# Exponentials written over the scores in PSUM, longer rings for halves and turned halves, w_out converted amid layer 1: cluster attention with two feed-forward layers on one core

## The chip, the cores and the metric

The kernel runs on one core of a Trainium2 chip. The metric is the device time of one execution in microseconds; the median of three runs stands for the kernel. A profiled execution is one more run with the hardware profiler on.

## What is computed

Attention in which a query sees only the keys of its own cluster, then a feed-forward layer with SiLU, then a second one with PReLU. Sizes: 2 batches, 8 heads, 768 rows, 64 columns a head, 16 clusters; the 1536 rows of 512 then pass through 512 x 2048 and 2048 x 512 twice. The weights arrive as 8-byte floats.

```python
q_assign = np.argmax(np.einsum('bhsd,hcd->bhsc', q_n, c_n), axis=-1)   # q_n, c_n: rows of length one
k_assign = np.argmax(np.einsum('bhsd,hcd->bhsc', k_n, c_n), axis=-1)
scores = scale * np.matmul(q, k.transpose(0, 1, 3, 2))
scores = np.where(q_assign[:, :, :, None] == k_assign[:, :, None, :], scores, -1000000000.0)
attn = np.exp(scores - np.max(scores, axis=-1, keepdims=True))
x = np.matmul(attn / (np.sum(attn, axis=-1, keepdims=True) + 1e-09), v)  # then heads side by side
h = x @ w_in;   x = (h * (1.0 / (1.0 + np.exp(-h)))) @ w_out             # first layer
h = x @ w2_in;  out = (np.maximum(h, 0.0) + alpha * np.minimum(h, 0.0)) @ w2_out
```

## The kernel before

Every number that enters a matmul is kept as two halves of 16 bits, a high and a low one, and each product is made of three matmuls (high by high, high by low, low by high).

Attention runs in 96 units, one for each tile of 128 rows and head: twelve tiles, eight heads. `front(u)` makes one unit's scores with four matmuls into one of two score buffers in PSUM (`bank_s`, two banks each; L804, L808). VectorE scales them in place and finds the extreme value (L818), ScalarE takes the exponential into one of two SBUF buffers of `p_buf` (L823), copies it to a high half (L830), and VectorE subtracts for the low half (L832; the list `P_LO_DVE` names the units that VectorE serves, all 96). The halves lie in one of two buffers (`o_hl`). `front_t(u)` has the DMA queue on SyncE turn them (L838) into one of three buffers (`o_pt`, `NPT`). `back(u)` multiplies them with the values (L850, 18 matmuls a unit, into `bank_x`). It is traced `LAG` units behind `front`, 2 here. After a tile's eighth unit `x_done` divides, splits and turns the tile's result (L870 to L881).

The first layer runs in seven chunks of one or two tiles (`CHUNKS`). `layer1(c)` makes eight groups of 24 matmuls against w_in (L1202), each with a Tanh on ScalarE (L1209) and passes of both engines behind it (L1210 to L1214), and then four groups of 48 matmuls against w_out (L1233). These groups take the two `w` banks of PSUM in turn; a third bank, `m`, joins once `w2_start` has been traced. Each weight is loaded in eight pieces, converted from 8-byte floats (L915 to L929), squared and summed (for the first layer by TensorE into a `w` bank, L964, read at L966), scaled by a common power of two (sums at L507, then L1048) and split into halves (L941, L942).

Weight preparation stands in a queue of tasks (`bg`). For the first layer it holds twelve tasks for w_in, four loads and eight conversions for w_out; `W_TASKS[u]` of them are traced behind unit u. `w1_finish` traces the rest, with w_out's scale and splits; it is called at step `W1_OUT_AT` = 16 of the first chunk. `UNITS_FIRST` says how many units are traced before the first chunk of layer 1; `UNITS_BY_CHUNK` how far attention has been traced at the end of each chunk. When all `NU + LAG` units are traced, `w2_start` queues the preparation of the second layer's weights, one task a step; their raw buffers lie where the keys were.

The order in which this is traced is not the order in which it runs. `Plan` takes all instructions with a cost for each and the data dependences between them (a PSUM tile counts as one cell), tries 61 orders with a seeded noise, and the one with the earliest end by its own count becomes the fixed order on every engine. What the traced order fixes is which buffer each use takes, and so which use has to wait for which.

Of the kernel before, what the change touches and what calls it, by code (L numbers as in the profile page):

```python
# [11 lines left out]
F32 = mybir.dt.float32  # L12
F16 = mybir.dt.float16
# [3 lines left out]
ACTF = mybir.ActivationFunctionType  # L17
ALU = mybir.AluOpType
# [3 lines left out]
CHUNKS = ((0, 1), (1, 1), (2, 2), (4, 2), (6, 2), (8, 2), (10, 2))  # L22


UNITS_FIRST = 17
UNITS_BY_CHUNK = (32, 53, 64, 69, 98, 98, 98)
W_TASKS = (
    2, 2, 2, 2, 1, 1, 1, 1, 2, 2, 2, 2, 2, 2, 2, 2,
    1, 1, 1, 1, 2, 2, 3, 2, 1, 1, 1, 1, 1, 1, 1, 1, 1, 1, 1, 1, 2, 2, 2, 2,
)  # L30
W2_TASKS = 1
W1_OUT_AT = 16
W_LOAD_AT = (0, 1, 3, 5)
# [5 lines left out]
V_SCALE_ON = ("papa", "appp")  # L39
SPLIT = ("aaaaaaaa", "aaaaaaaa", "aaaaaaaa", "aaaaaaaa")  # L40
EXP_ON = ("aaaaaaaa", "aaaaaaaa", "aaaaaaaa", "aaaaaaaa")
P_LO_DVE = range(96)

OUT_LAG = 2
READERS = 6
# [5 lines left out]
class Plan:  # L51
# [144 lines left out]

    def improve(self, rounds):

        noise = Random(3)
        found = [self.run(list(range(len(self.ins))))]  # L200
        back = self.mirror()
        for _ in range(rounds):
            back.run([noise.gauss(0, 0.1) - t for t in self.ended])
            found.append(self.run([noise.gauss(0, 0.1) - t for t in back.ended]))
        return min(found, key=lambda x: x[0])
# [128 lines left out]
def cluster_attention_silu_prelu(  # L334
# [20 lines left out]
    nc = tc.nc  # L355
    B, H, S, D = q.shape
# [7 lines left out]
    NC2 = 3  # L364
    N2 = NTILE * 128 // NC2

    NPT = 3
    NSTAT = 400
    NSCR = 128

# [1 line left out]
    KB = 1024  # L372
# [7 lines left out]
    def view(off, dt, *dims):  # L380
        n = 1
        for d in dims:
            n *= d
        nb = n * (2 if dt in (F16, BF16) else 4)
        assert off % 4 == 0 and nb % 4 == 0 and off + nb <= total, (off, nb)
        a = arena[:, off // 4:(off + nb) // 4]
        if dt != F32:
            a = a.bitcast(dt)
        if len(dims) == 1:
            return a  # L390
        names = [f"a{i}" for i in range(len(dims))]
        pat = f"p ({' '.join(names)}) -> p {' '.join(names)}"
        return a.rearrange(pat, **{n: d for n, d in zip(names, dims)})
# [3 lines left out]
    def region(nbytes):  # L397
        o = pos[0]
        pos[0] += nbytes
        return o  # L400
# [11 lines left out]
    o_qraw = region(4 * KB)  # L412
    o_kvraw = region(8 * KB)
    o_preq = region(4 * KB)
    o_p = region(6 * KB)
    o_hl = region(6 * KB)
    o_pt = region(NPT * 3 * KB)
    o_xhl = region(KB)
    o_xf = region(2 * KB)
# [13 lines left out]
    def col(n):  # L433
        a = stat[:, nstat[0]:nstat[0] + n]
        nstat[0] += n
        assert nstat[0] <= NSTAT
        return a
# [91 lines left out]
    def ring(name, n):  # L529
        i = ring_pos.get(name, 0)  # L530
        ring_pos[name] = i + 1
        return i % n

    def p_buf():
        return o_p + 3 * KB * ring("p", 2)


    half = small_p.tile([128, 12], F32, name="half")
    has = small_p.tile([128, B, H], F16, name="has")
# [60 lines left out]
    def load_kv(b, pr, which):  # L600
        return nc.sync.dma_start(
            out=view(kv_raw(b, pr)[which], F32, 2, T * D),
            in_=(k, v)[which][b, 2 * pr:2 * pr + 2].rearrange("h (p t) d -> p h (t d)", t=T),
        )
# [57 lines left out]
    def prep_v(b, pr):  # L662
        vr = view(kv_raw(b, pr)[1], F32, G, D)
        vt = view(o_v + 3 * KB * pr, F16, G, 2, D)
        nc.scalar.activation(out=vt[:, :, 0, :], in_=vr, func=ACTF.Copy)
        nc.gpsimd.tensor_tensor(out=vt[:, :, 1, :], in0=vr, in1=vt[:, :, 0, :], op=ALU.subtract)
        did.add(("v", b, pr))
        if pr == NP - 1:
            v_scales(b)
# [92 lines left out]
    def head_scales(n, pairs):  # L762

        b = n // T
        qt2 = view(o_qt + 4 * KB * (n % 2) + 2 * KB, F16, H, 128)
        d = d_cols[:, NP * (n % 2):NP * (n % 2) + NP]
        if pairs[0] == 0:
            (nc.gpsimd if n else nc.vector).tensor_scalar(
                d, isk[b], q_inv[:, n % 2:n % 2 + 1], 1.0 / float(D) ** 0.5 / MASK,
                op0=ALU.mult, op1=ALU.mult,  # L770
            )
        h0, nh = 2 * pairs[0], 2 * len(pairs)
        own = psum("m", nh)
        for i in range(nh):
            nc.tensor.matmul(
                out=own[:, i:i + 1], lhsT=qt2[0:D + C, h0 + i], rhs=has[0:D + C, b, h0 + i:h0 + i + 1],
                start=True, stop=True,
            )
        o = H * (n % 2) + h0
        nc.vector.tensor_tensor(  # L780
            out=nd_cols[:, o:o + nh].rearrange("p (a b) -> p a b", b=2),
            in0=own.rearrange("p (a b) -> p a b", b=2),
            in1=bc(d[:, pairs[0]:pairs[0] + len(pairs)], 2), op=ALU.mult,
        )
# [3 lines left out]
    sums = [col(H) for _ in range(2)]  # L788
# [5 lines left out]
    def front(u):  # L794
        n, h = divmod(u, H)
        b, pr = n // T, h // 2
        sc = bank_s[ring("s", 2)]
        qt1 = view(o_qt + 4 * KB * (n % 2), F16, H, 128)
        qt2 = view(o_qt + 4 * KB * (n % 2) + 2 * KB, F16, H, 128)
        kt1 = view(o_kt1 + 3 * KB * pr, F16, 2, T * 128)  # L800
        kt2 = view(o_kt2 + 3 * KB * pr, F16, 2, T * 128)
        hs = S // 2
        for j in range(2):
            nc.tensor.matmul(  # L804
                out=sc[:, j, :hs], lhsT=qt2[0:D + C, h],
                rhs=kt2[0:D + C, h % 2, j * hs:(j + 1) * hs], start=True, stop=False,
            )
            nc.tensor.matmul(  # L808
                out=sc[:, j, :hs], lhsT=qt1[:, h],
                rhs=kt1[:, h % 2, j * hs:(j + 1) * hs], start=False, stop=True,  # L810
            )
        if n % T == 0:
            if h % 2 == 0:
                head_scales(n, [pr])
        elif h == 0:
            head_scales(n, list(range(NP)))
        bias = un_cols[:, u % 3:u % 3 + 1]
        nc.vector.tensor_scalar(  # L818
            sc[:, :, :hs], sc[:, :, :hs], nd_cols[:, H * (n % 2) + h:H * (n % 2) + h + 1], None,
            op0=ALU.mult, op1=ALU.min, accum_out=bias,  # L820
        )
        o = p_buf()
        nc.scalar.activation(  # L823
            out=view(o, F32, 2, hs), in_=sc[:, :, :hs], func=ACTF.Exp, scale=-1.0, bias=bias,
            accum_out=sums[n % 2][:, h:h + 1],
        )
        p = view(o, F32, S)
        i = u % 2
        hl = view(o_hl + 3 * KB * i, F16, 2, S)
        nc.scalar.activation(out=hl[:, 0], in_=p, func=ACTF.Copy)  # L830
        en = nc.vector if u in P_LO_DVE else nc.gpsimd
        en.tensor_tensor(out=hl[:, 1], in0=p, in1=hl[:, 0], op=ALU.subtract)  # L832
        pt = view(o_pt + 3 * KB * (u % NPT), F16, 2 * T, 128)
        pt_of[u] = pt

    def front_t(u):
        hl = view(o_hl + 3 * KB * (u % 2), F16, 2 * S)
        nc.sync.dma_start_transpose(out=pt_of[u], in_=hl)  # L838

    def back(u):  # L840
# [221 lines left out]
    def run_bg(n):  # L1062
        for _ in range(n):
            if bg:
                bg.popleft()()
# [11 lines left out]
                f()  # L1077


    LAG = 2  # L1080
    NU = NTILE * H
    ready = set()
    g1_done = set()
# [1 line left out]
    def attention():  # L1085
# [36 lines left out]
        prep_v(0, 0)  # L1122
        for u in range(NU + LAG):
            n, h = divmod(u, H)
            if u < NU:
                front(u)
            if u >= LAG:
                back(u - LAG)
                if (u - LAG) % H == H - 1:
                    c = x_done((u - LAG) // H)  # L1130
                    if c is not None:
                        ready.add(c)
            if u < NU:
                front_t(u)
# [5 lines left out]
            for b in range(1, B):  # L1140
# [3 lines left out]
                for pr in range(NP):  # L1144
                    if at == (2 * pr - 2 if pr >= 2 else pr - 4):
                        load_kv(b, pr, 0)
                    if at == (2 * pr - 1 + LAG if pr else -2):
                        load_kv(b, pr, 1)
# [10 lines left out]
            if n + 1 < NTILE and n < NTILE:  # L1159
# [4 lines left out]
                if h == Q_AT[1]:  # L1164
                    prep_q_b(n + 1)
            run_bg(W_TASKS[u] if u < len(W_TASKS) else 0)
            yield u
# [365 lines left out]

    attend(UNITS_FIRST)
    while 0 not in ready:
        attend(done[0] + 1)
    steps = KF + 4 * KD
    for c in range(len(chunks)):
        while c not in ready:
            attend(done[0] + 1)  # L1540
        first = done[0]
        target = min(NU + LAG, UNITS_BY_CHUNK[c])
        steps_of = layer1(c)
        for i in range(steps):
            if c == 0:
                while i < KF and w1["in"].scales[i // 4] in bg:
                    run_bg(1)
                if i == W1_OUT_AT:
                    w1_finish()
            next(steps_of)  # L1550
            attend(first + (target - first) * (i + 1) // steps)
            if done[0] >= NU + LAG and not w2:
                w2_start()
            if w2:
                run_bg(W2_TASKS)
            if c == len(chunks) - 1 and i == KF + 4:
                split_x2(0)
        next(steps_of, None)
# [52 lines left out]
```

## Time and profile before

| | |
|---|---|
| median of 3 runs | 763.19 us (760.87 to 764.05) |
| the profiled execution | 764.79 us |
| its span, first to last instruction | 762.7 us |
| TensorE busy | 668.0 us (88%), 7035 matmuls |
| VectorE busy | 600.8 us (79%) |
| ScalarE busy | 483.8 us (63%) |
| GpSimd busy | 137.8 us (18%) |
| transposing DMAs | 149, median 3.9 us from issue to landing |
| loads of 8-byte weights | 32 of 1 MB, median 6.0 and 5.8 us to landing |

Busy time is not peak: matmuls are pipelined and their ends are modelled. A wait is put down to the releaser that came last by the profile. Idle time of an engine counts only where it is the one that the end waits for.

### The profile page before, as it was taken

How to read it: one execution, taken by the hardware profiler on the slowest of the kernel's cores; microseconds unless marked ns; L12 is line 12 of the kernel's file. 1: busy time of each engine (PE TensorE's matmuls, PEld its weight loads, DVE VectorE, ACT ScalarE, POOL GpSimd, SP SyncE). 2: the span in 40 equal slices, each digit the busy share in tenths (PEclk: the TensorE clock that was granted, in tenths of full speed). 3: DMA queues.
4: the chain of work that ended last, by engine and by line, in shares of the span. 5: the costliest groups of instructions: out<-in, count | busy, mean ns of one | idle time of the engine just before them, and what ended most of it. 6: DMA issues, size and time to landing. Idle time of an engine off the chain costs nothing.

```text
span 762.7 us, 17062 instructions
## 1 busy us (share of the span) xinstructions
PE 668.0 (88%) x7035; PEld 502.7 (66%) x7035; DVE 600.8 (79%) x1084; ACT 483.8 (63%) x779; POOL 137.8 (18%) x231
## 2 busy tenths in 40 slices
PE   0355568779999899999899999999999999999997
PEld 0243347668888788888788898884444687666653
DVE  4789999897679469867867885778999999966640
ACT  7978677877778557756765897888754532313111
POOL 4633042312232550321220101000000000000000
PEclk9995568899999999999999999999999999999999
DMA  7979997999989979988869875353200000001001
GB/s 223 315 191 271 295 274 156 143 164 162 180 161 160 151 139 161 157 155 141 146 117 149 191 176 137 146 214 126 111 1 0 28 28 1 2 1 56 1 0 56
DMA packets 237357, 100.86 MB, mean 132 GB/s; under 512 B 217312, under 2 KB 227552, under 8 KB 237280
## 3 DMA queue, kind: packets, MB, share of 16 engines
q1 hardware_dynamic: 237280, 99.78, 60.2%
q8 instruction: 55, 0.90, 0.5%
q14 instruction: 22, 0.18, 0.1%
HBM read 43.03 MB, written 3.15 MB: 61 GB/s over the span
## 4 chain that ended last, share of the span: by engine, by line
PE 41%; DVE 13%; DMA 9%; ACT 6%; issue 4%; POOL 1%; ACTq 0%; SPq 0%; POOLq 0%; DVEq 0%
PE s L1489 11%; PE w L1233 8%; PE w L1202 6%; PE w L1446 5%; DMA arena<-arena 4%; PE x L850 3%; DVE arena L942 3%; DMA arena<-in_moe_w_in_dram 3%; PE x L1446 2%; DMA arena<-in_moe_w_out_dram 2%; PE m L1446 2%; PE s L804 2%; PE s L808 2%; ACT arena L956 1%; DVE arena L1312 1%
## 5 line engine op out<-in xcount | busy, mean ns | idle before, releaser
L1233 PE MATMUL w<-arena 128*128 128x256 f16 (+1 forms) x1248 | 152.5, 259 | 5.2 <-DVE arena L942 4.3
L1202 PE MATMUL w<-arena 128*128 128x256 f16 (+1 forms) x1200 | 139.7, 258 | 2.7 <-DVE arena L1210 2.3
L1489 PE MATMUL s<-arena 128*128 128x512 f16 x576 | 134.3, 379 | 0.0
L1233 PEld LDWEIGHTS <-arena 128*128 128x128 f16 x1344 | 113.0, 99 | 24.0 <-DVE arena L942 5.2
L1202 PEld LDWEIGHTS <-arena 128*128 128x128 f16 x1344 | 113.4, 99 | 18.2 <-issue 3.9
L818 DVE TENSOR_SCALAR_CACHE_REDUCE s<-s,stat 128x768 f32<-128x768 f32 x96 | 97.9, 1021 | 21.4 <-PE s L808 15.1
L850 PE MATMUL x<-arena 128*128 128x64 f16 x1728 | 105.2, 198 | 7.6 <-DMA arena<-arena 7.6
L823 ACT ACTIVATE arena<-s,stat 128x768 f32<-128x768 f32 x96 | 86.0, 896 | 39.0 <-DVE s L818 19.9
L832 DVE TENSOR_TENSOR arena<-arena 128x768 f16<-128x768 f32 x96 | 94.6, 986 | 19.6 <-ACT arena L830 19.0
L850 PEld LDWEIGHTS <-arena 128*128 128x128 f16 x1728 | 88.7, 101 | 19.0 <-DMA arena<-arena 10.7
L1489 PEld LDWEIGHTS <-arena 128*128 128x128 f16 x576 | 56.3, 98 | 60.5
L830 ACT ACTIVATE arena<-arena 128x768 f16<-128x768 f32 x96 | 80.3, 839 | 21.7 <-DMA arena<-arena 21.3
L1406 ACT ACTIVATE arena<-arena,stat 128x512 f16<-128x512 f32 x48 | 33.7, 717 | 75.2 <-DVE arena L1403 75.1
L1446 PEld LDWEIGHTS <-arena 128*128 128x128 f16 x672 | 65.6, 98 | 15.6 <-issue 0.8
L804 PE MATMUL s<-arena 80*128 80x384 f16 x192 | 67.9, 356 | 8.3 <-ACT arena L823 5.7
L454 POOL TENSOR_SCALAR stat<-stat 128x1 int32<-128x1 int32 (+1 forms) x41 | 14.4, 355 | 324.8 <-DVE stat L449 220.5
L808 PE MATMUL s<-arena 128*128 128x384 f16 x192 | 68.1, 355 | 0.0
L942 DVE SCALAR_TENSOR_TENSOR arena<-arena,stat 128x1024 f16<-128x1024 f32 x40 | 51.5, 1306 | 9.0 <-ACT arena L941 9.0
L926 DVE SCALAR_TENSOR_TENSOR arena<-arena 128x1024 int32<-128x1024 int32 x32 | 39.2, 1224 | 24.6 <-ACT arena L919 24.5
L1446 PE MATMUL w<-arena 128*128 128x256 f16 x336 | 53.6, 273 | 0.4 <-ACT arena L1465 0.4
L941 ACT ACTIVATE arena<-arena,stat 128x1024 f16<-128x1024 f32 x40 | 45.7, 1173 | 11.2 <-DVE arena L1319 3.8
L915 ACT ACTIVATE arena<-arena 128x1024 int32<-128x1024 uint32 x32 | 36.8, 1151 | 22.2 <-DMA arena<-in_moe_w_out_dram 11.2
(176 smaller groups left out, 1076.6 us busy)
## 6 DMA issues: line engine op xcount, KB each, us to landing
arena<-in_moe_w_in_dram SPq DMA_DIRECT2D x16, 1024.0 KB, 6.0
arena<-in_moe_w_out_dram SPq DMA_DIRECT2D x16, 1024.0 KB, 5.8
arena<-in_k_dram SPq DMA_DIRECT2D x8, 384.0 KB, 3.9
arena<-in_q_dram SPq DMA_DIRECT2D x6, 512.0 KB, 5.5
arena<-in_v_dram SPq DMA_DIRECT2D x8, 384.0 KB, 6.2
out_dram<-arena SPq DMA_DIRECT2D x12, 256.0 KB, 2.1
arena<-arena SPq DMA_TRANSPOSE x149, 3.9
arena<-in_centroids_dram SPq DMA_DIRECT2D x1, 32.0 KB, 3.2
```

The costliest lines, as they stand in the source:

```text
L804: nc.tensor.matmul(out=sc[:, j, :hs], lhsT=qt2[0:D + C, h], rhs=kt2[0:D + C, h % 2, j * hs:(j + 1) * hs], start=True, stop=False,)
L808: nc.tensor.matmul(out=sc[:, j, :hs], lhsT=qt1[:, h], rhs=kt1[:, h % 2, j * hs:(j + 1) * hs], start=False, stop=True,)
L818: nc.vector.tensor_scalar(sc[:, :, :hs], sc[:, :, :hs], nd_cols[:, H * (n % 2) + h:H * (n % 2) + h + 1], None, op0=ALU.mult, op1=ALU.min, ...
L823: nc.scalar.activation(out=view(o, F32, 2, hs), in_=sc[:, :, :hs], func=ACTF.Exp, scale=-1.0, bias=bias, accum_out=sums[n % 2][:, h:h + 1],)
L830: nc.scalar.activation(out=hl[:, 0], in_=p, func=ACTF.Copy)
L832: en.tensor_tensor(out=hl[:, 1], in0=p, in1=hl[:, 0], op=ALU.subtract)
L850: nc.tensor.matmul(out=x_ps[0][:, h], lhsT=pt[:, ph * T + t], rhs=vt[:, h % 2, t, vh], start=(i == 0), stop=(i == 3 * T - 1),)
L942: nc.vector.scalar_tensor_tensor(out=lo, in0=t, scalar=s, in1=hi, op0=ALU.mult, op1=ALU.subtract)
L1202: nc.tensor.matmul(out=hp[:, ff], lhsT=wi[ff][:, a, kd], rhs=mov(bb, kd), start=(i == 0), stop=(i == 3 * KD - 1),)
L1233: nc.tensor.matmul(out=acc, lhsT=wo[:, a, f % 2, dt * 128:(dt + 1) * 128], rhs=g[:, f, bb], start=(i == 0), stop=(i == 3 * KF - 1),)
L1446: nc.tensor.matmul(out=hp[:, ff], lhsT=a_[:, a, kd, at + 128 * ff:at + 128 * ff + 128], rhs=b_[:, bb, kd], start=(k == 0), stop=(k == 5),)
L1489: nc.tensor.matmul(out=acc[t], lhsT=g[:, q, a, t * 128:(t + 1) * 128], rhs=wo[:, bb, f % 2], start=(first and q == 0 and k == 0), stop=(la ...
```

## The change

The buffers for exponentials go: the exponential is written over the scores in PSUM, and the copy and the subtraction read it there. There are three buffers for halves instead of two and four for turned halves instead of three; the value product is traced three units behind. The conversion of w_out is no longer traced during the first units: `W_TASKS` ends after ten units, with all of w_in and w_out's four loads, and the eight conversions follow one by one behind every second step of the first chunk's first half. That chunk is traced from unit 12 on instead of 17. The seed of the plan's noise is another. `UNITS_BY_CHUNK` stays, so that the last targets are 98 where all units traced make 99.

```diff
-UNITS_FIRST = 17
+UNITS_FIRST = 12
 UNITS_BY_CHUNK = (32, 53, 64, 69, 98, 98, 98)
-W_TASKS = (
-    2, 2, 2, 2, 1, 1, 1, 1, 2, 2, 2, 2, 2, 2, 2, 2,
-    1, 1, 1, 1, 2, 2, 3, 2, 1, 1, 1, 1, 1, 1, 1, 1, 1, 1, 1, 1, 2, 2, 2, 2,
-)
+W_TASKS = (2, 2, 2, 2, 1, 1, 1, 1, 2, 2)
...
-P_LO_DVE = range(96)
...
-        noise = Random(3)
+        noise = Random(1)
...
-    NPT = 3
+    NHL = 3
+    NPT = 4
...
-    o_p = region(6 * KB)
-    o_hl = region(6 * KB)
+    o_hl = region(NHL * 3 * KB)
     o_pt = region(NPT * 3 * KB)
...
-        o = p_buf()
+        p = sc[:, :, :hs]
         nc.scalar.activation(
-            out=view(o, F32, 2, hs), in_=sc[:, :, :hs], func=ACTF.Exp, scale=-1.0, bias=bias,
-            accum_out=sums[n % 2][:, h:h + 1],
-        )
-        p = view(o, F32, S)
-        i = u % 2
-        hl = view(o_hl + 3 * KB * i, F16, 2, S)
+            out=p, in_=p, func=ACTF.Exp, scale=-1.0, bias=bias, accum_out=sums[n % 2][:, h:h + 1]
+        )
+        hl = view(o_hl + 3 * KB * (u % NHL), F16, 2, 2, hs)
         nc.scalar.activation(out=hl[:, 0], in_=p, func=ACTF.Copy)
-        en = nc.vector if u in P_LO_DVE else nc.gpsimd
-        en.tensor_tensor(out=hl[:, 1], in0=p, in1=hl[:, 0], op=ALU.subtract)
+        nc.vector.tensor_tensor(out=hl[:, 1], in0=p, in1=hl[:, 0], op=ALU.subtract)
...
-        hl = view(o_hl + 3 * KB * (u % 2), F16, 2 * S)
+        hl = view(o_hl + 3 * KB * (u % NHL), F16, 2 * S)
         nc.sync.dma_start_transpose(out=pt_of[u], in_=hl)
...
-    LAG = 2
+    LAG = 3
...
             if c == 0:
                 while i < KF and w1["in"].scales[i // 4] in bg:
                     run_bg(1)
+                if i < W1_OUT_AT and i % 2:
+                    run_bg(1)
                 if i == W1_OUT_AT:
                     w1_finish()
```

## Rows read from the trace of the kernel before

**Rows 1.** The page's slices: busy tenths of TensorE, 40 equal slices.

```profile
PE   0355568779999899999899999999999999999997
```

**Rows 2.** Stretches: start and end, length, busy us and instructions of each engine, clock, DMA.

```profile
0.00:92.00 92.00, 36.64 (x437) 26.81 (x438) 71.53 (x174) 71.47 (x101) 34.69 (x71) 0.83 0.98 255
92.00:171.00 79.00, 59.93 (x857) 48.15 (x855) 74.07 (x144) 62.33 (x105) 22.44 (x29) 0.81 0.93 192
...
437.00:513.00 76.00, 72.95 (x772) 65.04 (x770) 54.47 (x75) 63.78 (x94) 6.26 (x22) 1.00 0.55 164
...
sum 762.00, PE 667.99 PEld 502.72 DVE 600.82 ACT 483.85 POOL 137.81; mean PE 83.50 PEld 62.84 DVE 75.10 ACT 60.48 POOL 17.23
```

**Rows 3.** The chain of waits from 437 us on: start, length, what it was.

```profile
436.88 7.92 DMA arena<-in_moe_w_in_dram
...
458.72 7.22 DMA arena<-in_moe_w_in_dram
```

**Rows 4.** Timeline of TensorE, first score matmuls of six units: start, length.

```profile
90.93 0.48 PE L804 MATMUL s<-arena 80*128 80x384 f16 x1
...
244.22 0.33 PE L804 MATMUL s<-arena 80*128 80x384 f16 x1
...
269.44 0.32 PE L804 MATMUL s<-arena 80*128 80x384 f16 x1
...
305.37 0.33 PE L804 MATMUL s<-arena 80*128 80x384 f16 x1
...
391.97 0.33 PE L804 MATMUL s<-arena 80*128 80x384 f16 x1
...
434.93 0.33 PE L804 MATMUL s<-arena 80*128 80x384 f16 x1
```

**Rows 5.** Line 1422: durations in ns, first and last start.

```profile
L1422 PE MATMUL x<-arena x48: 377/379/379, 514.4 to 551.6; 128*128 128x512 f16 x48
```

**Rows 6.** Timeline of TensorE, 117 to 145 us.

```profile
117.60 1.74 PE L1202 MATMUL w<-arena 128*128 128x128 f16 x20
...
137.86 0.34 PE L507 MATMUL w<-stat,arena 128*128 128x1 bf16 x8
...
144.76 0.39 PE L1233 MATMUL w<-arena 128*128 128x128 f16 x4
```

**Rows 7.** Timeline of VectorE, 117 to 146 us.

```profile
117.04 0.28 DVE L966 SCALAR_TENSOR_TENSOR arena<-w,arena 128x128 bf16<-128x128 f32 x1
...
123.64 0.28 DVE L966 SCALAR_TENSOR_TENSOR arena<-w,arena 128x128 bf16<-128x128 f32 x1
...
144.88 1.28 DVE L942 SCALAR_TENSOR_TENSOR arena<-arena,stat 128x1024 f16<-128x1024 f32 x1
```

**Rows 8.** Groups by line: count, busy us, mean ns, idle before and releasers.

```profile
L1202 PE MATMUL w<-arena 128*128 128x256 f16 (+1 forms) x1200 | 139.7, 258 | 2.7 <-DVE arena L1210 2.3 <-DMA arena<-arena 0.4
...
L850 PE MATMUL x<-arena 128*128 128x64 f16 x1728 | 105.2, 198 | 7.6 <-DMA arena<-arena 7.6
L818 DVE TENSOR_SCALAR_CACHE_REDUCE s<-s,stat 128x768 f32<-128x768 f32 x96 | 97.9, 1021 | 21.4 <-PE s L808 15.1 <-PE x L850 3.0 <-ACT arena L1240 1.6
L832 DVE TENSOR_TENSOR arena<-arena 128x768 f16<-128x768 f32 x96 | 94.6, 986 | 19.6 <-ACT arena L830 19.0
...
L823 ACT ACTIVATE arena<-s,stat 128x768 f32<-128x768 f32 x96 | 86.0, 896 | 39.0 <-DVE s L818 19.9 <-DVE arena L832 13.4 <-PE x L850 2.4
L830 ACT ACTIVATE arena<-arena 128x768 f16<-128x768 f32 x96 | 80.3, 839 | 21.7 <-DMA arena<-arena 21.3
...
L876 DVE TENSOR_TENSOR arena<-x,stat 128x512 f32<-128x512 f32 x12 | 8.2, 685 | 4.6 <-POOL arena L666 4.6
...
L1368 DVE TENSOR_TENSOR arena<-arena 128x512 f32<-128x512 f32 x8 | 5.4, 681 | 0.0
```

**Rows 9.** Timeline of VectorE, the subtractions of units 57 and 82.

```profile
309.96 0.96 DVE L832 TENSOR_TENSOR arena<-arena 128x768 f16<-128x768 f32 x1
...
401.45 0.95 DVE L832 TENSOR_TENSOR arena<-arena 128x768 f16<-128x768 f32 x1
```

More of the change, by code (lines that the diff above doesn't have):

```diff
@@ L532, in ring @@
         return i % n
-    def p_buf():
-        return o_p + 3 * KB * ring("p", 2)
     half = small_p.tile([128, 12], F32, name="half")
```

## The prediction

> **What bounds the kernel now.** I read the slices first: TensorE is idle for most of the first 170 us and nearly full from there to the end [rows 1]. The stretch table puts numbers on it: TensorE is busy 36.6 of the first 92 us and 59.9 of the next 79, so 74.4 us are idle by 171 us; of the 591.7 us that remain it is busy 571.4 (668.0 less those two), so only 20.3 us are idle there [rows 2]. In the early stretch the engine that is full is VectorE: 74.1 of the 79 us from 92 to 171 [rows 2]. It halves and scales sixteen weight pieces of layer 1 and at the same time serves the attention units. So the first bound is VectorE with its order of work, and the price of a bad order is idle TensorE.
>
> Second I read the chain of waits. From 436.9 us on it is no longer TensorE but the preparation of the second layer pair's weights: loads of 7.9 and 7.2 us, conversion, loads again [rows 3]. Those loads write where the keys lay, so they start when the last scores have been computed: the last unit's first score matmul is at 434.93 [rows 4]. The first product of the next stage follows at 514.4 [rows 5]. In between TensorE lives off layer 1 that is left over, and is busy 72.95 of 76 us [rows 2]. So the end hangs on two things that are nearly equally late: the sum of TensorE's work, and the end of attention plus a fixed tail of about 326 us (762.7 - 436.9). A gain reaches the end only if both move. That is what every step below is held against.
>
> **The change, part by part.** *1. w_out is converted amid layer 1 of the first chunk, and layer 1 is traced from unit 12 instead of 17.* Every order on an engine is planned anew from data dependences, so the traced order acts through shared buffers, above all the two w banks, used in turn. Before, the eight w_out conversions use them first, then the eight column groups of layer 1, then the sums for w_out's scale. The trace shows both fetters: the first layer-1 matmul starts at 117.60, just behind the read of a w_out square at 117.04 to 117.32 [rows 6, 7]; the last square is read at 123.64, but the sums for the scale run at 137.86, 14.2 us later, behind layer-1 groups, and with 7.0 us more the first w_out piece is split at 144.88 and TensorE starts the second half of the chunk at 144.76 [rows 6, 7]. In the new trace a conversion and a group alternate, so the conversions get one bank and the groups the other, and the scale's sums need only the last conversion. Up to 14.2 us of wait are gone. But VectorE has only 4.9 us free in this stretch [rows 2]: what is done earlier pushes attention units back. Bounds: 0 and 14.2 us; I take half, -7 us. The groups, now on one bank, each wait for the readers of the group before; those readers run on the full VectorE either way, so I cost it at nothing, and uncovered it comes out of the 14.2 us. [...]
>
> *2. Three buffers for halves, four for turned halves, values three units behind.* This removes waits on the transposing DMAs: TensorE's value matmuls wait 7.6 us on them, and ScalarE's copy into the halves 21.3 us, because its buffer is still being read [rows 8]. ScalarE is busy 484 of 763 us [rows 2], so its 21.3 us count only where they lengthen a unit. One more unit of distance should take about half of TensorE's: -4 us, bounds 0 and -7.6. The arena does not grow: 6 KB of buffers for exponentials go, 3 and 3 KB come.
>
> *3. Exponentials overwrite the scores.* The exponential now writes PSUM, the copy and the subtraction read it. No row shows ScalarE writing PSUM; the nearest are the copy inside SBUF (839 ns) and VectorE's pass in place in PSUM (1021 ns) against 896 ns now [rows 8], so -57 to +125 ns for each of 96. As ScalarE has room I take 0. The subtraction: a VectorE pass over 512 elements takes 685 ns with a PSUM operand and 681 without [rows 8], so 4 ns, under 0.4 us for 96. [...] The wait of the exponential for its own buffer (13.4 us of ScalarE behind the subtraction two units back [rows 8]) goes, but it does not vanish: it moves to the score matmul, which now must not start before the subtraction two units back has read the bank. Queued behind that matmul on TensorE is whatever the plan put there, layer 1 included. At today's pace this is the risk of the whole change; it is the slow rival below. In the sum I take 0.
>
> *4. The second pair's weights are traced one chunk later.* The test for the end of attention is 96 + 3 = 99 units now, while the targets of the last chunks stay at 98. So that preparation, and the third bank for layer 1 with it, begin with chunk 6 instead of chunk 5. The loads still need only the last scores, so the plan is free to start them as early. Chunk 5 has two banks: on the two w banks layer 1's first half waited 2.3 us on their readers in all [rows 8]. Cost 0 to 2.3, taken at +1 us. If the plan did start them late, the whole chain behind 436.9 us would shift with them.
>
> *5. A new seed, and the list of units whose low half VectorE computes.* The list held all 96 units, so nothing moves. The seed draws other candidate orders: bounds some 4 us to either side, a fifth of the 20.3 us that TensorE idles after 171 us [rows 2]; taken at 0.
>
> **The sum.** The profiled execution took 764.8 us (a span of 762.7 and 2.1 around it), 1.6 above the median of 763.2. 764.8 - 7 - 4 + 1 = 754.8, and against the median 753.2: I say 753 us. For that attention has to end some 10 us sooner as well; its own range is 746 to 759.
>
> **The rivals.** *Slower: the two score banks set attention's pace.* Unit 8's first score matmul is at 90.93, unit 95's at 434.93; without the pause of 25.2 us between units 47 and 48 (244.22 to 269.44), where the second batch's keys are not ready, that is 318.8 us for 86 steps, 3.71 us each [rows 4]. With two banks a unit may then hold its bank 7.41 us, from its first score matmul to the end of the subtraction. Today unit 57 needs 5.55 us (305.37 to 309.96 + 0.96) and unit 82 10.43 (391.97 to 401.45 + 0.95) [rows 4, 9]; nothing forces them to be short, since the bank is free after the exponential. The four passes alone take 1.02, 0.90, 0.84 and 0.99 us [rows 8], 3.75 us. From a mean hold of 7.41 us on, each further 0.1 us moves the end of attention by 86 x 0.05 = 4.3 us, and the tail of 326 us goes with it. At 7.7 us that is +12.5 us and the early gain is lost: 764.8 + 12.5 - 1.6 = 776 us. For it speaks that both engines of the chain are shared with layer 1; against it, that the passes follow each other without the buffer waits of part 2, and that the plan can fill TensorE with layer 1 meanwhile. [...]
>
> *Nothing moves.* VectorE is full before 171 us, so what the new order gives to w_out it takes from attention, and the tail still starts at 437: -2 for DMA waits, +1 for the bank: 762 us.
>
> *More than forecast.* All 14.2 us of part 1 and 7.6 of part 2 come, and attention, free of DMA waits, ends as much sooner: 764.8 - 21.8 - 1.6 = 741 us.
>
> **How the numbers follow.** The forecast gets 0.42, the slow rival 0.24, nothing 0.20, more 0.14. The range reaches to the rivals at either end, 740 to 778 us; about 0.16 is left outside. Half a per cent, about what a measurement of this kernel can tell from no change, is 3.8 us: faster means below 759.4, slower above 767.0. Faster: 0.38 of the forecast, 0.14, and 0.05 of "nothing": 0.57. Same: 0.04, 0.12 and 0.02 of the slow rival: 0.18. Slower: 0.22 and 0.03: 0.25.
>
> **What would show it.** Part 1: the sums for w_out's scale right behind the last square, within some 3 us instead of 14.2, layer 1's first matmul before 112 us, and TensorE busy clearly more than 59.9 us between 92 and 171. Part 2: waits of value matmuls and of the copy on transposes near zero. Part 3: the subtraction still at 0.95 to 1.0 us; score matmuls that wait for the subtraction instead of the exponential. Slow rival: holds near twice the unit's pace everywhere, and the last scores after 437 us. Part 4: the first load of the second pair's w_in within 10 us of the last scores. The forecast is wrong if attention ends later than 437 us, or if it ends sooner and the gap before the next stage's first product grows beyond 80 us.

## The result and the profile after

The changed kernel takes 756.44 us in the median of five runs (752.73 to 756.96), the kernel before 763.19: a ratio of 0.9906, with a 95% interval of 0.9877 to 0.9934. The profiled execution took 756.6 us, with a span of 754.8. The forecast was 753, in a range of 740 to 778. So the direction was right and the size about two thirds of the forecast (-6.8 us against -10.2 in the medians); the experiments show that the way there was not the forecast one.

The stretches of the kernel after, as in [rows 2] (start and end, length, busy us and instructions of TensorE, its weight loads, VectorE, ScalarE and GpSimd, clock, DMA):

```profile
0.00:92.00 92.00, 35.41 (x413) 25.71 (x413) 72.53 (x160) 72.16 (x101) 33.36 (x71) 0.84 0.96 271
92.00:171.00 79.00, 59.91 (x900) 48.58 (x901) 74.54 (x158) 61.79 (x108) 20.76 (x30) 0.84 0.97 178
...
437.00:513.00 76.00, 73.66 (x649) 60.62 (x648) 50.69 (x67) 55.79 (x80) 8.10 (x22) 1.00 0.39 129
513.00:600.00 87.00, 80.93 (x416) 39.65 (x414) 84.63 (x103) 53.00 (x72) 2.02 (x4) 1.00 0.16 55
```

Up to 171 us little was gained: TensorE is busy 95.3 us there, before 96.6, and at a granted clock of 0.84 instead of 0.83 and 0.81 it has done 1313 matmuls instead of 1294. The gain lies in the middle stretch, which is first of the kernel before and then of the kernel after:

```profile
171.00:437.00 266.00, 256.04 (x3506) 220.01 (x3504) 203.87 (x416) 186.27 (x338) 72.06 (x104) 0.99 0.89 155
```

```profile
171.00:437.00 266.00, 264.36 (x3675) 229.28 (x3673) 211.15 (x433) 197.48 (x357) 64.14 (x102) 1.00 0.93 167
```

TensorE's idle time in it falls from 10.0 to 1.6 us, and 169 more of its matmuls run in it. The groups of the attention chain after, as in [rows 8] (count, busy us, mean ns, idle before and releasers; line 838 is the value product, 810 the scaling, 820 the subtraction, 815 the exponential, 819 the copy, 796 the first score matmul):

```profile
L838 PE MATMUL x<-arena 128*128 128x64 f16 x1728 | 120.3, 196 | 7.3 <-DMA arena<-arena 7.3
L810 DVE TENSOR_SCALAR_CACHE_REDUCE s<-s,stat 128x768 f32<-128x768 f32 x96 | 97.6, 1021 | 24.3 <-PE s L800 23.2 <-PE x L838 0.4
L820 DVE TENSOR_TENSOR arena<-s,arena 128x768 f16<-128x768 f32 x96 | 91.4, 953 | 13.0 <-ACT arena L819 12.6
L815 ACT ACTIVATE s<-s,stat 128x768 f32<-128x768 f32 x96 | 83.9, 873 | 56.0 <-DVE s L810 49.2 <-DVE stat L447 4.2 <-DVE stat L445 2.2
L819 ACT ACTIVATE arena<-s 128x768 f16<-128x768 f32 x96 | 77.5, 809 | 1.7 <-DMA arena<-arena 0.3
L796 PE MATMUL s<-arena 80*128 80x384 f16 x192 | 68.0, 354 | 12.6 <-DVE arena L820 11.1 <-DMA arena<-arena 1.4
```

Three things are to be seen. ScalarE's copy waited 21.3 us on transposes and now waits 0.3. The value product waited 7.6 and still waits 7.3. And the score matmul, which waited for the exponential, now waits 11.1 us for the subtraction. Its row before:

```profile
L804 PE MATMUL s<-arena 80*128 80x384 f16 x192 | 67.9, 356 | 8.3 <-ACT arena L823 5.7 <-DMA arena<-arena 2.5
```

Timeline of TensorE after, the first score matmuls of units 8, 47, 48, 82 and 95, beside [rows 4]:

```profile
95.56 0.48 PE L796 MATMUL s<-arena 80*128 80x384 f16 x1 [0.78 <-DVE arena L820]
...
232.97 0.33 PE L796 MATMUL s<-arena 80*128 80x384 f16 x1
...
251.83 0.33 PE L796 MATMUL s<-arena 80*128 80x384 f16 x1
...
378.70 0.33 PE L796 MATMUL s<-arena 80*128 80x384 f16 x1
...
421.81 0.33 PE L796 MATMUL s<-arena 80*128 80x384 f16 x1
```

Unit 8 starts 4.6 us later than before, the pause between the batches is 18.9 us instead of 25.2, and the other 86 steps take 3.57 us each instead of 3.71 ((421.81 - 95.56 - 18.86) / 86). Together the last scores are 13.1 us earlier, at 421.81 instead of 434.93. From there to the end of the span, the tail, it takes 333.0 us instead of 327.8, so 7.9 us of the 13.1 reach the end.

### The profile page after: what moved, and what is told of

Read it like the earlier page. It is cut to its first block, busy times and chain, and to the rows that moved or that the text cites. A ratio compares the mean times of both kernels' runs of the same rounds, so it can differ in the third digit from the quotient of the medians.

```text
span 754.8 us, 17044 instructions
## 1 busy us (share of the span) xinstructions
PE 663.7 (88%) x7035; PEld 500.2 (66%) x7035; DVE 598.3 (79%) x1084; ACT 482.2 (64%) x779; POOL 128.7 (17%) x231
## 4 chain that ended last, share of the span: by engine, by line
PE 46%; DVE 13%; DMA 6%; ACT 4%; issue 3%; POOL 2%; ACTq 0%; POOLq 0%
PE s L1477 11%; PE w L1190 10%; PE w L1221 9%; PE x L838 4%; PE w L1434 4%; DVE arena L930 3%; DMA arena<-in_moe_w_out_dram 3%; PE s L796 2%; PE s L800 2%; DMA arena<-in_moe_w_in_dram 2%; PE x L1434 2%; PE m L1434 2%; DVE arena L1300 1%; DVE arena L917 1%; DVE arena L914 1%
## 5 line engine op out<-in xcount | busy, mean ns | idle before, releaser
L1190 PE MATMUL w<-arena 128*128 128x256 f16 (+1 forms) x1272 | 152.7, 258 | 3.6 <-DMA arena<-arena 2.3
L1221 PE MATMUL w<-arena 128*128 128x256 f16 (+1 forms) x1296 | 154.1, 257 | 1.6 <-DVE arena L1198 1.1
L1477 PE MATMUL s<-arena 128*128 128x512 f16 x576 | 136.1, 379 | 1.4 <-DVE arena L930 1.4
L838 PE MATMUL x<-arena 128*128 128x64 f16 x1728 | 120.3, 196 | 7.3 <-DMA arena<-arena 7.3
L815 ACT ACTIVATE s<-s,stat 128x768 f32<-128x768 f32 x96 | 83.9, 873 | 56.0 <-DVE s L810 49.2
L820 DVE TENSOR_TENSOR arena<-s,arena 128x768 f16<-128x768 f32 x96 | 91.4, 953 | 13.0 <-ACT arena L819 12.6
L796 PE MATMUL s<-arena 80*128 80x384 f16 x192 | 68.0, 354 | 12.6 <-DVE arena L820 11.1
L819 ACT ACTIVATE arena<-s 128x768 f16<-128x768 f32 x96 | 77.5, 809 | 1.7 <-DMA arena<-arena 0.3
L450 POOL TENSOR_SCALAR stat<-stat 128x1 int32<-128x1 int32 (+1 forms) x41 | 11.6, 286 | 307.0 <-DVE stat L445 210.1
L1434 PE MATMUL w<-arena 128*128 128x256 f16 x336 | 56.5, 273 | 0.0
```

The lines of the kernel that those rows point to most:

```text
L796: nc.tensor.matmul(out=sc[:, j, :hs], lhsT=qt2[0:D + C, h], rhs=kt2[0:D + C, h % 2, j * hs:(j + 1) * hs], start=True, stop=False,)
L815: nc.scalar.activation(out=p, in_=p, func=ACTF.Exp, scale=-1.0, bias=bias, accum_out=sums[n % 2][:, h:h + 1])
L820: nc.vector.tensor_tensor(out=hl[:, 1], in0=p, in1=hl[:, 0], op=ALU.subtract)
L838: nc.tensor.matmul(out=x_ps[0][:, h], lhsT=pt[:, ph * T + t], rhs=vt[:, h % 2, t, vh], start=(i == 0), stop=(i == 3 * T - 1),)
L1190: nc.tensor.matmul(out=hp[:, ff], lhsT=wi[ff][:, a, kd], rhs=mov(bb, kd), start=(i == 0), stop=(i == 3 * KD - 1),)
L1221: nc.tensor.matmul(out=acc, lhsT=wo[:, a, f % 2, dt * 128:(dt + 1) * 128], rhs=g[:, f, bb], start=(i == 0), stop=(i == 3 * KF - 1),)
```

## The experiments

Each kernel was timed in five rounds beside runs of the kernel before on the same chip. The median of before moved between 762.4 and 764.2 us from one set of runs to the next, so the ratios with their 95% intervals are compared. A bound on what small differences mean: every edit makes the plan draw a new order, and a new seed alone (e7, below) moved the time by 0.3%. So the differences of 0.3 and 0.4% named below can be the new order as well as the edit; the 1.1 to 1.8% that the rings are worth (after against e4, e8 against e3, e1 against e5) are several times that. With values two units behind, all units traced make 98, so in those kernels the second pair's weights are also traced from the end of chunk 4 again (part 4); e10 has that change by itself.

| kernel | buffers for halves / turned halves / values behind | exponential in | w_out amid layer 1 | seed | ratio to before | last unit's scores at, us | copy waits on transposes, us |
|---|---|---|---|---|---|---|---|
| before | 2 / 3 / 2 | SBUF, two | no | 3 | 1 | 434.9 | 21.3 |
| after | 3 / 4 / 3 | PSUM | yes | 1 | 0.9906 (0.9877 to 0.9934) | 421.8 | 0.3 |
| e1 | 3 / 4 / 3 | PSUM | no | 1 | 0.9895 (0.9869 to 0.9922) | 423.3 | 1.7 |
| e8 | 3 / 4 / 3 | PSUM | no | 3 | 0.9883 (0.9857 to 0.9910) | 423.4 | 2.1 |
| e10 | 3 / 4 / 3, last targets 99 | PSUM | no | 1 | 0.9910 (0.9876 to 0.9944) | 425.3 | 0.6 |
| e11 | 3 / 4 / 3, squares in bank m | PSUM | yes | 1 | 0.9948 (0.9926 to 0.9970) | 427.1 | 1.1 |
| e6 | 3 / 3 / 2 | PSUM | no | 1 | 0.9935 (0.9911 to 0.9958) | 425.9 | 2.9 |
| e12 | 4 / 3 / 2 | PSUM | no | 1 | 0.9888 (0.9846 to 0.9929) | 422.2 | 1.1 |
| e9 | 3 / 3 / 2 | SBUF, one | no | 1 | 0.9951 (0.9924 to 0.9978) | 433.2 | 0 |
| e2 | 2 / 3 / 2 | SBUF, two | yes | 3 | 1.0041 (1.0021 to 1.0061) | 433.5 | 21.5 |
| e7 | 2 / 3 / 2 | SBUF, two | no | 1 | 1.0033 (1.0012 to 1.0053) | 436.4 | 31.6 |
| e3 | 2 / 3 / 2 | PSUM | no | 3 | 1.0034 (1.0014 to 1.0054) | 437.9 | 21.5 |
| e4 | 2 / 3 / 2 | PSUM | yes | 1 | 1.0020 (1.0000 to 1.0040) | 436.7 | 26.5 |
| e5 | 2 / 4 / 3 | PSUM | no | 1 | 1.0073 (1.0045 to 1.0101) | 442.6 | 21.8 |

The table divides by one column: the eight kernels with three or four buffers for halves are all faster than before, and of the five with two none is.

### Which part carries it

*e1: w_out's conversion back into the first units.*

```diff
-UNITS_FIRST = 12
+UNITS_FIRST = 17
-W_TASKS = (2, 2, 2, 2, 1, 1, 1, 1, 2, 2)
+W_TASKS = (
+    2, 2, 2, 2, 1, 1, 1, 1, 2, 2, 2, 2, 2, 2, 2, 2,
+    1, 1, 1, 1, 2, 2, 3, 2, 1, 1, 1, 1, 1, 1, 1, 1, 1, 1, 1, 1, 2, 2, 2, 2,
+)
...
-                if i < W1_OUT_AT and i % 2:
-                    run_bg(1)
```

> The kernel after, with w_out's conversion traced during the first units again and the first chunk from unit 17 (the seed stays 1). Theory A, the gain is made after 171 us by attention that no longer waits for its buffers: 757 us, TensorE idle under 3 us between 171 and 437 us, last scores near 422 us. Theory B, the gain comes from the first chunk: 763 us. In either case the sums for w_out's scale fall back to 12 to 14 us behind the last square.

*e2: only that part, on the kernel before* (the diff of e1 the other way round).

> The kernel before, with only w_out's conversion traced amid the first chunk and that chunk from unit 12. Theory A: 763 us, within 2 of the kernel before; the sums for the scale right behind the last square, and still TensorE busy 60 us between 92 and 171. Theory B: 757 us.

*e3: only the exponential over the scores, on the kernel before.*

```diff
-        o = p_buf()
+        p = sc[:, :, :hs]
...
-            out=view(o, F32, 2, hs), in_=sc[:, :, :hs], func=ACTF.Exp, scale=-1.0, bias=bias,
-            accum_out=sums[n % 2][:, h:h + 1],
+            out=p, in_=p, func=ACTF.Exp, scale=-1.0, bias=bias, accum_out=sums[n % 2][:, h:h + 1]
...
-        p = view(o, F32, S)
...
-        hl = view(o_hl + 3 * KB * i, F16, 2, S)
+        hl = view(o_hl + 3 * KB * i, F16, 2, 2, hs)
```

> The kernel before, with only the exponential written over the scores in PSUM; two buffers for halves, three for turned halves, values two units behind. Theory A1, the longer rings carry the gain: the score banks are held longer while the copy still waits for its buffer, 764 to 770 us, the copy's waits on transposes still near 20 us. [...]

*e4: the kernel after without the longer rings* (the room stays the same).

```diff
-    NHL = 3
-    NPT = 4
+    NHL = 2
+    NPT = 3
-    LAG = 3
+    LAG = 2
```

> The kernel after with two buffers for halves, three for turned halves and values two units behind. Theory A1: 763 us or more, the copy's waits on transposes back near 20 us. [...]

Measured: e1 0.9895, e2 1.0041, e3 1.0034, e4 1.0020. Theory B is out: without w_out amid layer 1 the whole gain stays, and that part alone gains nothing (0.4% slower). In e1 the sums for w_out's scale run at 141.45, 21.3 us behind the read of the last square, where I expected 12 to 14, and it makes no difference to the end. Theory A holds, and A1 in it: writing in place without the rings is slower by 0.3%, and the kernel after without the rings has no gain. The copy's line in e1 and in e3 (durations in ns, first and last start; below, what ScalarE's idle time before it waited for and how often):

```profile
L822 ACT ACTIVATE arena<-s x96: 783/811/857, 44.3 to 428.5; 128x768 f16<-128x768 f32 x96
...
  DMA arena<-arena: 1.7, 3
```

```profile
L828 ACT ACTIVATE arena<-s x96: 783/811/863, 45.9 to 450.5; 128x768 f16<-128x768 f32 x96
...
  DMA arena<-arena: 21.5, 28
```

### Which ring

*e5 and e6: e1 with two buffers for halves, and e1 with three buffers for turned halves and values two units behind* (the room stays the same).

```diff
-    NHL = 3
+    NHL = 2
```

```diff
-    NPT = 4
+    NPT = 3
-    LAG = 3
+    LAG = 2
```

> The kernel of e1_no_w (753.6 us) with two buffers for halves; four for turned halves and values three units behind stay. Theory H, the third buffer for halves carries the gain, since the copy no longer waits for the transpose two units back: 762 us, the copy's waits on transposes back above 15 us. Theory T, the distance of the values carries it: 754 us.

> The kernel of e1_no_w with three buffers for turned halves and values two units behind; three buffers for halves stay. Theory H: 754 to 756 us, the copy's waits under 5 us. Theory T: 762 us, the value matmuls' waits on transposes clearly above 12.7 us.

*e12: e6 with its free room given to a fourth buffer for halves* (`NHL = 4`).

> The kernel of e6_pt3 (ratio 0.9935 to before) with a fourth buffer for halves in the same room that e1_no_w gives to the fourth for turned halves; values stay two units behind. If three buffers for halves already cover the transpose, and what e1 gains over e6 comes from the distance of the values: 0.992 to 0.995, the copy's waits near zero, the value matmuls' waits still well above e1's 12.7 us. If any further room in the chain will do: 0.988 to 0.991.

Measured: e5 1.0073, e6 0.9935, e12 0.9888. Theory H holds for e5, which is even slower than the 762 us expected: one buffer for halves is worth 1.8% here (e5 against e1, 769.5 against 753.6 us with befores of 764.2 and 762.4). The copy in e5:

```profile
L822 ACT ACTIVATE arena<-s x96: 785/810/867, 43.1 to 449.0; 128x768 f16<-128x768 f32 x96
...
  DMA arena<-arena: 21.8, 24
```

What such a wait holds up is to be seen at unit 37 of e5. First ScalarE (822 is the copy, 818 the exponential, 1200 the Tanh of layer 1), then TensorE (799 is the first score matmul, 823 the subtraction):

```profile
213.31 0.63 ACT L732 ACTIVATE arena<-arena 128x512 f16<-128x512 f32 x1
216.58 0.81 ACT L822 ACTIVATE arena<-s 128x768 f16<-128x768 f32 x1 [2.64 <-DMA arena<-arena]
217.28 0.87 ACT L818 ACTIVATE s<-s,stat 128x768 f32<-128x768 f32 x1
...
218.16 0.69 ACT L1200 ACTIVATE arena<-w,stat 128x512 f32<-128x512 f32 x1
```

```profile
218.43 0.32 PE L799 MATMUL s<-arena 80*128 80x384 f16 x1 [0.54 <-DVE arena L823]
```

The next unit's scores were scaled at 215.75, but its exponential runs behind the copy that waits for a transpose, the Tanh behind that, and the score matmul of unit 39 waits for unit 37's subtraction, that is, for its bank.

For e6 the signs of both theories came: the copy waits 2.9 us, but the value matmuls with their weight loads wait 39.9 us on transposes (12.7 in e1), and 758.7 us lies between the two forecasts. The fourth buffer for turned halves with the larger distance gives some 0.4% on top (e6 against e1; the intervals overlap a little), and a fourth buffer for halves, with the values two units behind, as much (e12 against e6; these overlap too). So my expectation for e12, that only the distance of the values would do, was wrong: the time is that of e1, and the value matmuls' waits fall to 19.3 us. That any further room behind the copy will do is likely by this, but not clear of the noise. A single buffer short at one place, as in e5, is not made up for by room at the next.

### The seed

*e7 and e8: the kernel before with the other seed, and e1 with the seed of before.*

```diff
-        noise = Random(3)
+        noise = Random(1)
```

> The kernel before with the other seed alone. If the drawn order is worth little, as the sum had it (0, bounds 4 us to either side): 759 to 767 us, last scores at 434 to 438 us. If the seed carries the gain: 757 us or less.

> The kernel of e1_no_w with the seed of before: write in place and longer rings, nothing else. If the seed is worth little: 751 to 757 us. If the seed carried part of the gain: 759 us or more.

Measured: e7 1.0033, e8 0.9883. The drawn order does not carry the gain: on the kernel before the new seed costs 0.3%, and with write in place and rings both seeds are within each other's intervals. With one seed, 3, the parts can be read off one after the other: before 1, with the exponential in place 1.0034, with the rings too 0.9883. The rings are worth 1.5%, some 11.5 us of 763 (with part 4, which goes with the larger distance and shows no price in e10), and they take the 6 KB that the first step frees. The rings without it were not tried, for want of room; e9, below, has the third buffer for halves without it, in exchange for one of the two buffers for exponentials.

### The hold of the score banks, the late weights, the single bank

*e9: e6 with the exponential in one SBUF buffer instead of PSUM*, so that a score bank is free after the exponential.

```diff
-    o_pt = region(12 * KB)
+    o_pt = region(9 * KB)
+    o_p = region(3 * KB)
...
-        p = sc[:, :, :hs]
+        p = view(o_p, F32, 2, hs)
...
-            out=p, in_=p, func=ACTF.Exp, scale=-1.0, bias=bias, accum_out=sums[n % 2][:, h:h + 1]
+            out=p, in_=sc[:, :, :hs], func=ACTF.Exp, scale=-1.0, bias=bias, accum_out=sums[n % 2][:, h:h + 1]
```

> The kernel of e6_pt3 (758.7 us) with the exponential written into one SBUF buffer instead of over the scores: the same three buffers for halves, the same three for turned halves, values two units behind. If the longer hold of the score banks costs time, this gives it back: 755 us or less, score matmuls no longer waiting for the subtraction. If the hold is free and one buffer for exponentials fetters as much: 757 to 762 us, the exponential waiting for the subtraction one unit back.

Measured: 0.9951, against 0.9935 for e6, with intervals that overlap. The copy's wait for transposes is gone here too, and the exponential waits for the subtraction of the unit before:

```profile
L819 ACT ACTIVATE arena<-s,stat x96: 875/900/988, 39.8 to 445.1; 128x768 f32<-128x768 f32 x96
...
  DVE arena L824: 38.0, 49
```

So with three buffers for halves a gain is there even with a single buffer for exponentials in SBUF, though the last scores come at 433.2 us, only 1.7 us sooner than before. That the longer hold costs time is not seen: without it the kernel is not faster. Whether one buffer and the hold cost nothing, or just cost the same, this run does not tell.

*e10: e1 with the last three targets at 99*, so that the second pair's weights are traced from the end of chunk 4 again.

```diff
-UNITS_BY_CHUNK = (32, 53, 64, 69, 98, 98, 98)
+UNITS_BY_CHUNK = (32, 53, 64, 69, 99, 99, 99)
```

> The kernel of e1_no_w (753.6 us) with the last three targets at 99, so that the second pair's weights are traced from the end of chunk 4 again. If tracing them one chunk later costs what the sum had (1 us, 0 to 2.3): 751 to 754 us. If it costs nothing, within 1 us of e1.

Measured: 0.9910, against 0.9895 for e1; the intervals overlap, and no gain is seen.

*e11: the kernel after with w_out's squares and their sum in bank m*, so that the first chunk's groups have both w banks.

```diff
-        w1["out"] = out_tasks(w1_out, raws, o_ts, o_w + 32 * KB, w1["in"], "w", SPLIT[1], EXP_ON[1])
+        w1["out"] = out_tasks(w1_out, raws, o_ts, o_w + 32 * KB, w1["in"], "m", SPLIT[1], EXP_ON[1])
```

> The kernel after with the sums of squares and of the scale of w_out made in the bank m, so that layer 1's groups of the first chunk have both w banks. Theory G, w_out amid layer 1 costs 3 us because these groups queue on one bank: 753 to 754 us, and TensorE busier than 59.9 us between 92 and 171. Theory V, VectorE is full and the order gives nothing: 755 to 757 us.

Measured: 0.9948, slower than either theory had it; the interval just overlaps that of the kernel after. Theory G got no support: TensorE is busy 59.88 us between 92 and 171. But the run does not settle it, since bank m has its own queue (the sums of the query preparation), and the last w_out square came at 141 us instead of 123.7. What the single bank costs stays open.

## Why the prediction came out as it did

**Part 1, w_out amid layer 1: forecast -7 us, measured nothing.** The mechanism came as written, the worth did not. Timeline of TensorE after, beside [rows 6] (line 1190 is the first half of layer 1, 952 the squares, 503 the sums, 1221 the second half):

```profile
120.11 1.33 PE L1190 MATMUL w<-arena 128*128 128x128 f16 x11 [2.31 <-DMA arena<-arena]
...
123.71 0.62 PE L952 MATMUL w<-arena 128*128 128x128 bf16 x8
125.35 0.34 PE L503 MATMUL w<-stat,arena 128*128 128x1 bf16 x8
...
130.77 0.28 PE L1221 MATMUL w<-arena 128*128 128x128 f16 x2
```

And of VectorE, beside [rows 7] (954 reads the square, 930 splits the first piece of w_out):

```profile
124.37 0.29 DVE L954 SCALAR_TENSOR_TENSOR arena<-w,arena 128x128 bf16<-128x128 f32 x1 [0.52 <-PE w L952]
...
131.85 1.28 DVE L930 SCALAR_TENSOR_TENSOR arena<-arena,stat 128x1024 f16<-128x1024 f32 x1
```

The sums follow the square within 1.0 us instead of 14.2, and the first split and the second half start 13 and 14 us earlier. Yet TensorE is as busy between 92 and 171 us as before (59.91 and 59.93), with 900 matmuls instead of 857. The step that failed is the choice of half the bound: the lower bound, zero, was the right value, and its reason stood in the same paragraph, a VectorE that is busy 74 of 79 us. It is busy 74.5 of 79 after. Other work came later: the last of the eight groups on one bank starts at 156.7 us, before at 139.5, and unit 8 starts 4.6 us later. Layer 1's first matmul came at 120.11, not before 112 as I wrote; it waited for the turned rows of the first tile. That the full VectorE did this, and not the single bank, which I had costed at nothing, is argued and not shown, since e11 does not separate the two. e2 has this part's price alone, +0.4%, and e1 against the kernel after shows none that can be told from zero.

**Part 2, the rings: forecast -4 us, measured -11.5.** The term was sized from the wrong row. I took half of TensorE's 7.6 us, because TensorE is the engine that is full; that wait is still 7.3. (I also read the matmuls' row alone; with their weight loads it is 18.2 us before and 16.6 after.) The 21.3 us on ScalarE's copy I set aside, since ScalarE is busy only 63% of the time. That row pointed at the cause, the missing third buffer for halves: e5 takes the buffer away, the wait is back at 21.8 us, and with it the time. What stands behind a waiting copy waits too, the next exponential and layer 1's Tanh among it, and a score bank stays occupied meanwhile, as unit 37 of e5 shows (2.64 us idle before the copy, 0.54 us before the score matmul). The row does not give the size: e7 waits 31.6 us and e3 21.5, with equal times, and e9 waits 0 and is only 0.5% faster than the kernel before. The busy share of ScalarE, 63%, said little here about what a wait on it costs, as the engine is a link in a chain that runs 96 times.

**Part 3, the exponential in place: forecast 0, measured +0.3% alone, and the room for part 2.** The subtraction's price was right: 953 ns with a PSUM operand and 957 without in the median (953 and 986 on average). The slow rival was real, but not in the kernel after. From each unit's first score matmul to the end of its subtraction, averaged over units 8 to 95, the hold is 6.48 us after, under the 7.41 that I gave as the point from which it decides; unit 82 has 378.70 to 383.73:

```profile
382.77 0.96 DVE L820 TENSOR_TENSOR arena<-s,arena 128x768 f16<-128x768 f32 x1
```

In e3, e4 and e5, with two buffers for halves, it is 7.34, 7.30 and 7.21 us, and the last scores come at 437.9, 436.7 and 442.6 us, later than before. There the copy sits on the bank while it waits for its buffer. But 7.41 us is two steps of the kernel before; held against two steps of its own (twice 3.74, 3.79, 3.97 and 3.57 us, worked out as above), the hold is 98% in e3, 96% in e4, 91% in e5 and 91% in the kernel after. So the hold and the rings hang together, and in e3 and e4 the two banks may set the pace; in e5, the slowest, that is not shown.

**Part 4, later weights: forecast +1 us, nothing seen** (e10). The first loads of the second pair's w_in are issued at 416.45 and 423.69 us, within 10 us of the last scores at 421.81, as forecast. Unlike what I wrote, the first of them does not need the very last scores: it is issued 5.4 us ahead of them, and 7.9 us in the kernel before (427.05).

**Part 5, the seed: forecast 0 with 4 us to either side.** e7 gives +0.33%, 2.5 us; e8 against e1 no difference.

**The sum.** -10 us were forecast on the profiled execution and -8.2 measured, by a term of -7 that was not there and a term of -4 that was -11.5. The range of 746 to 759 that I gave the sum is not what the bounds of its terms add up to, 741 to 766 without the seed; the measured time lies in both. That the end hangs on the last scores held in the main, but the tail is not fixed: over all profiles here it is 324 to 334 us, a spread larger than the gain, so with last scores at 433.2 and 433.5 us e9 is faster than before and e2 slower. The condition I set, that both TensorE's sum and the end of attention have to move, was too strict: in e1 TensorE is busy 667.4 us, about as long as before (668.0), and the gain is idle time.

Of the 13.1 us by which the last scores came sooner 5.2 were given back in that tail, though the gap from them to the next stage's first product fell from 79.4 to 73.8 us. In the stretch from 513 to 600 us TensorE idles 6.1 us, before 2.1:

```profile
513.00:600.00 87.00, 84.90 (x418) 39.81 (x417) 84.38 (x104) 53.79 (x73) 2.02 (x4) 1.00 0.16 61
```

The chain of waits runs there through the loads of the second pair's w_out, first of the kernel before and then of the kernel after:

```profile
494.27 5.65 DMA arena<-in_moe_w_out_dram
...
509.66 7.29 DMA arena<-in_moe_w_out_dram
...
522.16 4.92 DMA arena<-in_moe_w_out_dram
```

```profile
488.27 7.09 DMA arena<-in_moe_w_out_dram
...
503.80 6.37 DMA arena<-in_moe_w_out_dram
...
520.25 5.05 DMA arena<-in_moe_w_out_dram
...
531.97 6.50 DMA arena<-in_moe_w_out_dram
```

The first load of w_in is issued 10.6 us sooner than before, the first load of w_out only 6.0. So part of the lead is lost before w_out's turn, while w_in is loaded and converted; what takes it is not shown.

e1 and e8 have tails of 328.0 and 329.1 us with last scores only 1.5 us later, and with e12 they have the lowest ratios here. Their intervals overlap with that of the kernel after, so it is not shown that they beat it; leaving w_out where it was loses nothing that can be seen.

## What to carry to other kernels

Where a chain of several engines runs many times, look for the wait in its middle that is for a free buffer, not only for waits on the engine that is full: here 21 us of an engine with a third of its time to spare stood for 11 us of the end. Such a row says where to look; what it is worth takes a run with one more buffer. Before paying for an earlier start of one step, see which engine is full in that stretch; if it is full, as VectorE is here with 74.1 of 79 us, an earlier step can be another one's delay, and zero is the safer value. And an operand that can stay in PSUM may be worth nothing by itself and much by the SBUF that it frees; here two banks bore it, with a mean hold of 6.48 us at 3.57 us a unit.

## What the runs showed of the hardware

ScalarE's passes were a little shorter where PSUM stands in place of SBUF: the exponential takes 875 ns in place in PSUM in the kernel after, against 900 from PSUM to SBUF in the kernel before (medians), and the copy 811 ns from PSUM against 838 from SBUF. The subtraction takes up to 1399 ns before and up to 1779 in e9, with both operands in SBUF, and never more than 959 in the kernel after, with one in PSUM:

```profile
L832 DVE TENSOR_TENSOR arena<-arena x96: 906/957/1399, 46.1 to 450.6; 128x768 f16<-128x768 f32 x96
```

```profile
L824 DVE TENSOR_TENSOR arena<-arena x96: 937/955/1779, 46.9 to 448.8; 128x768 f16<-128x768 f32 x96
```

```profile
L820 DVE TENSOR_TENSOR arena<-s,arena x96: 940/953/959, 48.8 to 430.0; 128x768 f16<-128x768 f32 x96
```

In the kernel before 12 subtractions take 1000 ns or more, and beside each of them a GpSimd instruction runs; the other 84 stay at 960 or less, 19 of them beside one. In the kernel after 34 of the 96 run beside a GpSimd instruction, and none takes more than 959 ns. So in these two kernels every long one has both operands in SBUF and a GpSimd neighbour. That the neighbour lengthens it was not shown: no run here took GpSimd's work away.
